# A retention layer and its MLP: the state cleared by VectorE, and a new order for the early tasks

## The chip, the cores and the metric

The kernel runs on one core of a Trainium2 chip. The metric is the device time of one execution in microseconds; of several executions the median counts. A profile is one execution recorded by the hardware: it shows when each instruction of each engine started and how long it took. The engines are TensorE (PE, matrix products), VectorE (DVE), ScalarE (ACT), GpSimd (POOL) and SyncE (SP, here only an issuer of transfers). They run side by side and wait for each other through semaphores. Matmuls write to PSUM banks; everything else is in SBUF.

## The reference

Two layers, one after the other. The first is a retention layer over 4 batches, 8 heads, 768 steps and head width 64; each head decays its state by its own factor:

```python
for t in range(S):
    state = gamma[None, :, None, None] * state + np.einsum('bhd,bhe->bhde', k[:, :, t], v[:, :, t])
    y[:, :, t] = scale * np.einsum('bhd,bhde->bhe', q[:, :, t], state)
```

with `gamma = 1 - 2**(-5 - h)` and `scale = 1/sqrt(64)`. Its output, with the heads side by side, is x (4 x 768 x 512). The second layer normalises each row of x and sends it through an MLP:

```python
xn = (x - mu) / np.sqrt(var + 1e-06) * g_ln
ch = np.maximum(xn @ w_ch1, 0.0) @ w_ch2
return (x + ch).astype(np.float32)
```

w_ch1 is 512 x 2048, w_ch2 is 2048 x 512.

## The kernel before

**Tiles.** The 768 steps of a batch are cut into 6 chunks of 128. A tile t is one chunk c of one batch b, with all heads. The 24 tiles come in the order of `TILES` (line 190): tiles 0 to 3 are chunk 0 of the four batches, 4 to 8 are chunks 1 to 5 of batch 0, and so on. Retention is computed chunk by chunk. Within a chunk it is a masked product of q and k with v; what earlier chunks hand on is a state per head, 64 x 64, kept for all heads in two alternating tiles `state[0]` and `state[1]` of 128 x 512 bf16 (line 275). Only the two diagonal blocks of each pair of heads are ever written, so the rest of both tiles must be zero: `c_zero` (line 339) clears them once.

**The steps of a tile**, by the names used below (t is the tile, the engine in brackets):
- tk, tq (PE, lines 498, 505): k and q are transposed into the banks b0 and b1. trk (ACT, 256) and trq (DVE, 510, scaled by decay) copy them out. From tile 8 on a DMA transpose takes the place of tk and tq.
- pa (PE, 538): the product of trk and trq. asb (DVE, 562): pa times the decay mask.
- y (PE, 586, and 582 for what comes from the state): asb times v.
- bn (DVE, 601 and 602): mean and variance of each row of y. xn (DVE, 613): y less its mean, times g_ln. x_all (ACT, 619): a copy of y, which reads its bank after xn.
- tx (PE, 672): xn is transposed. xnt (ACT, 256) copies it out for the MLP.
- vg (POOL, 633), pd (PE, 645) and the state update (DVE, 659, two instructions): v with decay, its product with k summed in PSUM, and the scaled sum put into a state tile. Tile t of chunk c needs the update of chunk c - 1 of its batch.
- Sqrt (ACT, 694) and the reciprocal (DVE, 700) give 1/sigma, which is needed only when the MLP's result is added.

**The MLP.** Tiles are taken in groups: eight of one tile, four of two, two of four. The first product, m1(g, n), runs over quarter n of group g's hidden width (line 719; 16 matmuls of 128 x 128 for a group of one tile) into one of two buffers named mm; a relu (line 732 on ACT, 734 on DVE) empties it into h1. Quarter n uses the part w1_n of the first weights. The second product (line 757, m2) takes h1 into a bank and line 767 adds x.

**What sets the order.** Each step is a task, made by `plan.add` in `Plan` (line 86) and numbered as it is made. `ORDER` (lines 29 to 69) lists all 866 tasks; each engine takes its own in that order and never passes a waiting one. Where a number is 10000 or more, the ten thousands digit picks the second engine that may do the task and the hundred thousands digit the second bank. `Plan.order` walks the list with planned durations and landing times (`w_pad` is one of these: ns added to the planned landing of a weight load). From its planned starts `Plan.fill` (line 145) puts matmuls on zeros (line 785) into the gaps that it expects on TensorE before 14 us, to keep TensorE busy. By its arithmetic there are 25 of these, the last ahead of y of tile 1.

**Loads.** GpSimd issues the loads of q, k, v (line 430) and of the weights (line 438) in one queue; each casts from fp32 to bf16. k and q of tile 0 come in by SyncE's and ScalarE's queues and are cast by ScalarE and VectorE (line 256). From tile 9 on small copies by GpSimd (line 447) hold a load back until an earlier one has landed.

**Where the clear stands.** Task 13 (`zerod`, line 359) is on GpSimd, behind the load of w1_2 and ahead of vg of tile 0. The first state update (216) waits for it.

Of the kernel before, what the change touches and what calls it, by code (L numbers as in the profile page):

```python
# [14 lines left out]
PE, ACT, DVE, POOL, SP = range(5)  # L15
# [4 lines left out]
              "k3", "q3", "v3", "w1_2", "k4", "q4", "v4", "k5", "q5", "v5", "w1_3", "w2_0",  # L20
              "k6", "q6", "v6", "k7", "q7", "v7", "w2_1", "w2_2", "w2_3"],
    "bufs": {"qsb": 6, "ksb": 5, "vsb": 9, "qk": 8, "tr": 6, "vg": 3, "trq": 3, "trk": 3},
    "load_pad": 600, "w_pad": 1500, "lead": 32, "lead2": 32, "sq_at": 28000, "late_load": 1700, "two": 4, "m2b": ("b0",), "m2all": 16, "inter": 4, "every": 4, "tail": (0, 384, 512), "step": 8, "pace": 8, "ahead": 3,
    "slack": 600, "tr_pad": 4000, "x_pad": 3500, "vg_pad": 2500, "fill": 0.8, "fill_end": 14000,
}

ORDER = [int(x) for x in """
16 17 2 0 3 19 20 23 14 8 15 1 24 5 7 9 25 4 10 6 21 11 26 18 22 146 45 100147 149 148  # L30
27 150 28 151 153 46 162 100163 29 152 154 164 165 30 155 12 166 31 156 167 32 157 158
159 47 168 176 13 524 169 179 214 100177 170 525 33 215 178 171 172 216 180 34 173 181
532 35 526 36 533 182 37 190 527 534 183 193 38 100191 184 535 48 192 185 186 194 187
195 49 540 542 541 196 204 543 528 197 39 207 100205 198 536 529 40 200 42 43 41 206 544
50 217 234 52 51 53 10537 55 208 100224 54 199 201 545 550 209 225 548 551 210 227 44
226 251 202 549 552 228 218 56 211 546 553 547 222 275 212 219 538 229 235 220 100241
554 539 530 10555 221 213 242 244 531 243 230 231 556 560 57 174 557 258 561 245 261 236
232 233 558 100237 562 238 246 259 247 10559 260 566 563 564 567 262 252 570 203 248 249
254 565 188 255 568 60 250 569 263 100722 160 61 58 59 268 62 287 253 298 63 723 716 724
301 66 264 67 64 717 65 725 269 718 161 571 175 189 719 265 726 266 720 576 100271 270  # L40
276 307 267 578 272 579 577 239 728 273 68 69 278 277 72 729 730 731 318 73 279 70 299
71 280 580 572 732 281 300 282 74 322 284 223 286 734 735 75 288 581 283 285 736 302 303
290 289 573 737 291 738 574 319 584 292 740 741 293 320 294 296 742 308 304 240 585 78
575 743 582 744 295 297 310 333 79 76 309 77 339 586 305 583 311 80 746 587 334 747 312
335 313 314 274 316 323 81 256 315 748 84 350 749 351 588 592 317 325 85 82 83 379 750
589 257 324 354 326 727 602 86 752 87 753 327 328 329 603 593 590 754 755 594 591 330 90
331 340 352 332 342 756 341 343 721 380 598 321 599 595 91 758 336 759 344 760 761 596
733 88 345 89 355 762 346 368 348 353 600 92 757 745 739 337 597 347 93 764 96 349 97 94
381 601 95 765 98 338 357 604 356 766 606 386 99 605 382 607 767 358 306 359 383 614 612
768 360 384 615 361 613 363 770 397 102 771 103 100 362 772 398 365 364 763 369 101 104  # L50
371 370 773 403 610 372 608 774 611 373 776 616 609 399 366 105 374 387 108 109 617 375
618 414 367 377 106 107 777 620 418 751 376 378 389 619 110 388 778 390 779 622 415 391
385 404 780 392 393 621 623 630 782 395 111 114 429 115 631 394 112 400 456 113 433 626
116 624 117 396 406 120 121 416 405 430 783 627 625 407 784 431 408 628 419 409 634 785
410 629 632 411 412 457 118 119 122 413 421 635 786 445 633 420 123 788 126 458 422 127
789 646 124 423 424 790 425 427 647 401 125 426 428 791 642 638 434 436 792 435 794 795
796 639 643 465 769 437 438 640 417 439 440 442 128 797 459 641 129 441 446 443 476 132
644 798 432 402 133 645 636 130 448 447 648 131 134 138 637 460 650 449 450 649 800 651
461 451 452 801 802 477 454 803 444 775 480 462 453 466 478 455 135 491 804 136 137 468
492 467 806 139 495 807 469 470 140 493 808 471 141 809 472 142 474 473 475 652 653 654  # L60
481 483 482 484 810 655 656 658 143 510 479 485 144 787 506 805 657 799 145 659 660 661
486 662 507 496 487 489 664 663 488 508 490 666 498 497 665 499 667 668 670 669 500 671
501 502 672 673 504 511 812 674 503 505 676 513 512 675 514 678 463 677 680 515 679 682
813 681 814 683 516 494 811 509 517 781 519 464 518 520 815 100830 831 816 521 832 818
819 200824 820 825 684 817 793 685 826 690 688 691 827 689 694 696 833 695 522 686 697
687 708 709 821 698 699 692 693 523 822 848 700 828 834 702 100842 701 703 706 707 704
200836 714 837 705 715 712 838 849 843 713 710 711 850 844 845 839 846 851 840 100854
852 855 856 823 847 841 835 829 853 857 860 861 858 862 863 864 859 865
""".split()]


# [90 lines left out]
def kernel(  # L162
# [16 lines left out]
    nc = tc.nc  # L179
# [158 lines left out]

    def c_zero(eng):
        for x in state:  # L340
            nc.gpsimd.memset(x, 0.0)

    a = plan.add
    small = a(DVE, 1200, -100, c_small)
# [11 lines left out]
    qscd = a(ACT, 700, -91, c_qsc, [args, table])  # L356
    maskd = a(DVE, 1230, -50, c_mask, [vscd, tri])
    gchd = a(ACT, 900, 100, c_gch, [small, qscd, vscd], at=9000)
    zerod = a(POOL, 500, 0, c_zero, at=9000)
    exps = [gchd, qscd, vscd]  # L360

    def c_gb(eng):
# [101 lines left out]
    for g in range(NG):  # L464
        for ho in range(HO):
            unit["1", g, ho] = u
            u += GROUPS[g] / 4
            every = CFG["every"] if GROUPS[g] == 1 else 8 if 12 <= G0[g] < 16 and GROUPS[g] == 2 else 4
# [239 lines left out]
    for g in range(NG):  # L708
        n = GROUPS[g]
        hb, h0 = buf_of[g]  # L710
        two = GMAX // n
# [109 lines left out]
```

## Time and profile before

| | before |
|---|---|
| median of 5 runs | 215.87 us (215.34 to 217.04) |
| profiled execution, its own time | 217.04 us |
| span from its first to its last instruction | 215.3 us |
| TensorE busy | 206.8 us, 96% |
| VectorE, ScalarE, GpSimd busy | 119.6, 86.4, 97.0 us |
| mean granted clock of TensorE | 0.999 |
| first layer of the MLP, line 719 | 896 matmuls, 95.2 us |
| second layer, line 757 | 379 matmuls recorded, 88.4 us |
| matmuls on zeros, line 785 | 24 recorded, 8.0 us |
| clear of the state, line 341 | 2 on GpSimd, 1.01 us, from 14.14 us |

The profiled execution was the slowest of the five. A few matmul records are missing from a trace, so counts on TensorE can be a little low. In a timeline a row is a run of instructions of one line: start, time from the first start to the last end, engine, line, what it writes and reads, how many, and in brackets how long the engine was idle before it and what ended that. Matmuls overlap, so the time from one row's start to the next says more about cost than the time of a row. Busy TensorE counts from issue to drain in the same way.

### The profile page before, as it was taken

To read this page: it belongs to the slowest core of one execution; us is meant where nothing else is said; L and a number is where in the kernel's file an instruction comes from. 1 tells how busy PE (TensorE), PEld (TensorE's weight loads), DVE (VectorE), ACT (ScalarE), POOL (GpSimd) and SP (SyncE) were. 2 spreads that over 40 slices of the span, in tenths; PEclk is the share of its full clock that TensorE was granted. 3 is DMA by queue.
4 is the path that set the end of the run, shared out by engine and by line. 5 is a ranking of instruction groups with operands and counts; after the bars stand their busy time and mean duration, and the time that the engine had idled before them with its cause. 6 is when DMAs were issued, how large, how long until landed. Compare 5 with 4: busy or idle time off the path is not lost.

```text
span 215.3 us, 4941 instructions
## 1 busy us (share of the span) xinstructions
PE 206.8 (96%) x2005; PEld 131.8 (61%) x2027; DVE 119.6 (56%) x260; ACT 86.4 (40%) x175; POOL 97.0 (45%) x151
## 2 busy tenths in 40 slices
PE   7998899999999999999999999999999999999992
PEld 3368799994666667665676776674445444444452
DVE  5477667872667774863684677478686510030041
ACT  5246678652412324343333542261366601544200
POOL 8968697529778475755675648221000000000000
PEclk9999999999999999999999999999999999999999
DMA  9999999999999999999999999939440260000035
GB/s 128 168 180 180 165 191 178 205 114 117 105 112 128 122 128 171 142 261 158 88 172 165 105 170 121 151 73 125 98 155 20 56 191 3 0 0 0 0 144 200
DMA packets 108890, 26.85 MB, mean 125 GB/s; under 512 B 101569, under 2 KB 105921, under 8 KB 108866
## 3 DMA queue, kind: packets, MB, share of 16 engines
q0 software_dynamic: 77024, 13.37, 82.0%
q1 hardware_dynamic: 27186, 6.59, 21.9%
q10 hardware_dynamic: 4656, 6.56, 8.8%
q8 instruction: 16, 0.26, 0.5%
q14 instruction: 8, 0.07, 0.1%
HBM read 27.30 MB, written 6.29 MB: 156 GB/s over the span
## 4 chain that ended last, share of the span: by engine, by line
PE 91%; ACT 2%; DMA 2%; DVE 2%; issue 1%; ACTq 0%; DVEq 0%
PE b L757 38%; PE mm L719 38%; PE pa L538 3%; PE pd L645 2%; DMA osb<-in_q_dram 2%; PE pd L785 2%; PE b L572 2%; PE b L548 2%; PE mm L364 1%; PE b L586 1%; PE b L498 1%; DVE xn L613 1%; PE b L505 1%; DVE bns L601 1%; PE b L672 1%
## 5 line engine op out<-in xcount | busy, mean ns | idle before, releaser
L719 PE MATMUL mm<-xnt,w 128*128 128x128 bf16 (+2 forms) x896 | 95.2, 257 | 0.9 <-ACT xnt L256 0.8
L757 PE MATMUL b<-w,h 128*128 128x512 bf16 (+2 forms) x379 | 88.4, 370 | 1.2 <-issue 0.2
L732 ACT ACTIVATE h<-mm 128x512 bf16<-128x512 f32 x93 | 55.0, 598 | 83.6 <-PE mm L719 83.3
L719 PEld LDWEIGHTS <-w 128*128 128x128 bf16 x896 | 66.1, 98 | 21.3 <-issue 1.0
L757 PEld LDWEIGHTS <-h 128*128 128x128 bf16 x400 | 37.0, 98 | 37.7
L562 DVE TENSOR_TENSOR asb<-pa,mask 128x1024 bf16<-128x1024 f32 x24 | 29.4, 1224 | 21.0 <-PE pa L538 20.5
L767 DVE SCALAR_TENSOR_TENSOR osb<-b,rstd,x_all 128x512 f32<-128x512 f32 (+2 forms) x25 | 18.0, 727 | 27.3 <-PE b L757 27.0
L601 DVE BATCH_NORM_STATS2 bns<-b 128x6 f32<-128x256 f32 (+1 forms) x40 | 17.8, 477 | 17.7 <-PE b L572 11.0
L619 ACT CAST x_all<-b 128x256 bf16<-128x256 f32 (+1 forms) x40 | 16.2, 417 | 23.1 <-DVE xn L613 18.9
L613 DVE SCALAR_TENSOR_TENSOR xn<-b,mv,gb 128x256 bf16<-128x256 f32 (+1 forms) x40 | 20.1, 532 | 0.8
L633 POOL TENSOR_TENSOR vg<-vsb,vsc 128x512 bf16<-128x512 bf16 x16 | 16.6, 1049 | 7.8 <-PE pd L645 7.5
L430 POOL DMA_DIRECT2D vsb<-in_v_dram x20 | 18.1, 905 | 2.1 <-DMA qsb<-in_q_dram 1.3
L659 DVE TENSOR_TENSOR state<-pd,gch 64x256 bf16<-64x256 f32 x40 | 16.6, 414 | 3.4 <-PE pd L645 2.6
L430 POOL DMA_DIRECT2D qk<-in_q_dram x16 | 14.2, 887 | 2.4 <-issue 2.4
L430 POOL DMA_DIRECT2D qk<-in_k_dram x16 | 14.3, 892 | 1.2 <-issue 1.1
L447 POOL COPY scrap<-qk 1x1 bf16<-1x1 bf16 x30 | 5.8, 192 | 19.1 <-DMA qk<-in_q_dram 10.5
L700 DVE RECIPROCAL rstd<-rstd 128x1 f32<-128x1 f32 (+2 forms) x14 | 2.0, 157 | 13.4 <-ACT rstd L694 13.4
L785 PE MATMUL pd<-zeros 128*128 128x512 bf16 (+1 forms) x24 | 8.0, 487 | 1.3 <-DVE zeros L291 1.2
L438 POOL DMA_DIRECT2D w<-in_moe_w_ch_dram x8 | 6.2, 776 | 4.0 <-DMA w<-in_moe_w_ch_dram 4.0
L572 PEld LDWEIGHTS <-asb 128*128 128x128 bf16 x128 | 5.8, 98 | 2.4
L447 POOL COPY scrap<-vsb 1x1 bf16<-1x1 bf16 x15 | 2.6, 176 | 9.5 <-DMA vsb<-in_v_dram 9.4
L527 DVE TENSOR_TENSOR trq<-tr,qsc 128x512 bf16<-128x512 bf16 x16 | 6.7, 418 | 0.1
(68 smaller groups left out, 130.2 us busy)
## 6 DMA issues: line engine op xcount, KB each, us to landing
out_dram<-osb ACTq DMA_DIRECT2D x23, 256.0 KB, 3.4
w<-in_moe_w_ch_dram POOLq DMA_DIRECT2D x8, 512.0 KB, 10.3
vsb<-in_v_dram POOLq DMA_DIRECT2D x20, 128.0 KB, 5.2
qk<-in_k_dram POOLq DMA_DIRECT2D x16, 128.0 KB, 4.5
qk<-in_q_dram POOLq DMA_DIRECT2D x16, 128.0 KB, 5.1
qsb<-in_q_dram POOLq DMA_DIRECT2D x7, 128.0 KB, 9.2
v<-in_v_dram POOLq DMA_DIRECT2D x4, 128.0 KB, 7.7
ksb<-in_k_dram POOLq DMA_DIRECT2D x4, 128.0 KB, 9.2
```

Source lines behind the costliest of these rows:

```text
L430: nc.gpsimd.dma_start(out=tile_of(kind, j), in_=src)
L562: nc.vector.tensor_tensor(out=take("asb", t, [P, NPAIR, 2, P], BF16).rearrange("p i a t -> p a i t"), in0=held["pa", t], in1=mask.rearrang ...
L601: nc.vector.bn_stats(out=bns[:, t, i, :], in_=x)
L613: nc.vector.scalar_tensor_tensor(out=dst, in0=src, scalar=mv[:, t, 0:1], in1=g, op0=ALU.subtract, op1=ALU.mult)
L619: nc.scalar.copy(out=dst, in_=src)
L633: e.tensor_tensor(out=take("vg", j, [P, H, D], BF16), in0=tile_of("v", j), in1=vsc[:, cc, :].unsqueeze(2).to_broadcast([P, H, D]), op=ALU. ...
L659: nc.vector.tensor_tensor(out=held["pb", n][o, :, o], in0=held["pd", b][o, :, o], in1=gch[o, cc, :].unsqueeze(2).to_broadcast([D, NPAIR, D ...
L719: nc.tensor.matmul(p[:, j, :], lhsT=w1[:, ko, (ho + j) * P:(ho + j + 1) * P], rhs=held["xnt", hb][:, h0:h0 + n, ko, :], start=(ko == 0), s ...
L732: nc.scalar.activation(out=dst, in_=src, func=AF.Relu)
L757: nc.tensor.matmul(held[key][:, 0:w], lhsT=held["h1", hb][:, ho, i * P:(i + 1) * P], rhs=w2[:, ho, cols], start=(ho == 0), stop=(ho == HO ...
L767: nc.vector.scalar_tensor_tensor(out=take("osb", key, [P, w], FP32), in0=held[key][:, 0:w], scalar=rstd[:, t:t + 1], in1=x_all[:, t, cols] ...
L785: nc.tensor.matmul(held["pd", "warm"][:, 0:w], lhsT=zeros[:, 0:P], rhs=zeros[:, 0:w], start=True, stop=True)
```

## The change

It has three parts.

1. The clear of the two state tiles is made by VectorE instead of GpSimd, and its task stands behind the making of the causal triangle (task 6) and ahead of the cast of q of tile 0 (task 21). GpSimd goes from the load of w1_2 straight to vg of tile 0.
2. `w_pad` goes from 1500 to 550.
3. `ORDER` is new for the first tasks, most of it up to tile 8 (the last to move is a Sqrt, 256, in the time of tile 10); after that both lists are the same. No task is added or left out. Per engine:

- TensorE. From tq of tile 2 on, before: tq2, pd of tile 0 (215), tx1, pa2, m1(1,0) (532), m1(0,1) (526), y2, tk3, m1(1,1) (534), tq3, tx2, pa3, m1(2,0) (540), m1(2,1), y3, tk4, m1(0,2), tq4, m1(1,2), tx3. After: tq2, tx1, pa2, 532, 215, y2, 534, tk3, 526, tq3, tx2, pa3, 540, m1(2,1), y3, tk4, m1(1,2), tq4, m1(0,2), tx3. Up to tq2 nothing moves. From tile 4 to tile 7 steps of the chain and matmuls of the MLP change places with neighbours.
- ScalarE. The decay factors of the state (task 12, line 337) stand ahead of the copy of g_ln's rows and of trk1, where they stood behind them. The first Sqrt, which also loads the table for it, was 202 (group 3), behind trk of tile 5; it is now 160 (group 0), between xnt of tile 0 and trk of tile 2. The other Sqrts are spread out behind it. The relu of m1(0,0) (525) goes behind xnt1. For tiles 2 and 3 xnt goes ahead of x_all. Some relus change between ScalarE and VectorE: 527, 529, 549, 531 and 561 to VectorE, and 537, 555 and 559 to ScalarE.
- VectorE. The first state update (216) stood between trq2 and asb2; it now stands behind asb3. Of the reciprocals, 161 (group 0) goes ahead of trq3. The later state updates of batch 0 change places with neighbours.
- GpSimd. Besides the clear, vg of tile 7 (268) goes ahead of the issue of q of tile 9, behind which it stood.

```diff
@@ CFG @@
...
-    "load_pad": 600, "w_pad": 1500, "lead": 32,
+    "load_pad": 600, "w_pad": 550, "lead": 32,
...
@@ ORDER @@
-16 17 2 0 3 19 20 23 14 8 15 1 24 5 7 9 25 4 10 6 21 11 26 18 22 146 45 100147 149 148
-27 150 28 151 153 46 162 100163 29 152 154 164 165 30 155 12 166 31 156 167 32 157 158
-159 47 168 176 13 524 169 179 214 100177 170 525 33 215 178 171 172 216 180 34 173 181
-532 35 526 36 533 182 37 190 527 534 183 193 38 100191 184 535 48 192 185 186 194 187
-195 49 540 542 541 196 204 543 528 197 39 207 100205 198 536 529 40 200 42 43 41 206 544
-50 217 234 52 51 53 10537 55 208 100224 54 199 201 545 550 209 225 548 551 210 227 44
-226 251 202 549 552 228 218 56 211 546 553 547 222 275 212 219 538 229 235 220 100241
-554 539 530 10555 221 213 242 244 531 243 230 231 556 560 57 174 557 258 561 245 261 236
-232 233 558 100237 562 238 246 259 247 10559 260 566 563 564 567 262 252 570 203 248 249
-254 565 188 255 568 60 250 569 263 100722 160 61 58 59 268 62 287 253 298 63 723 716 724
-301 66 264 67 64 717 65 725 269 718 161 571 175 189 719 265 726 266 720 576 100271 270
-276 307 267 578 272 579 577 239 728 273 68 69 278 277 72 729 730 731 318 73 279 70 299
-71 280 580 572 732 281 300 282 74 322 284 223 286 734 735 75 288 581 283 285 736 302 303
-290 289 573 737 291 738 574 319 584 292 740 741 293 320 294 296 742 308 304 240 585 78
...
+16 17 2 0 3 19 20 23 14 8 15 1 24 5 7 9 25 4 10 6 13 21 11 26 18 45 22 27 146 28 149
+100147 148 150 46 29 151 30 162 100163 153 12 152 165 154 164 166 155 31 156 157 167 32
+158 168 169 47 100176 159 170 524 177 178 160 179 100172 214 180 181 171 173 532 33 215
+182 183 525 184 534 161 190 533 193 34 35 36 526 100191 186 535 192 194 10527 187 540 37
+38 185 542 195 48 196 49 39 541 216 197 204 40 42 43 41 536 198 50 217 543 207 234
+100205 206 528 537 200 52 51 201 544 199 208 10529 224 209 545 552 188 548 10549 553 174
+100225 210 227 550 551 546 53 55 175 226 228 211 54 212 44 218 219 547 213 554 530 220
+555 251 202 221 235 100241 229 538 230 56 244 10531 236 556 539 242 275 231 558 100258
+557 232 559 243 560 10561 237 562 57 245 246 233 238 239 563 222 566 259 564 247 260 567
+248 189 261 570 262 252 565 568 249 60 254 255 250 569 223 253 203 263 100722 61 268 58
+59 62 287 298 63 723 716 724 301 66 67 64 717 65 264 725 269 718 571 719 265 726 266 270
+720 576 100271 276 307 267 578 272 579 577 728 273 68 69 278 277 72 729 730 731 318 73
+279 70 299 71 280 580 572 732 281 300 282 74 322 284 286 734 735 75 288 581 283 285 736
+302 303 290 289 573 737 291 738 574 319 584 292 740 741 293 320 294 296 742 308 304 240
...
@@ c_zero and its task @@
     def c_zero(eng):
         for x in state:
-            nc.gpsimd.memset(x, 0.0)
+            nc.vector.memset(x, 0.0)
...
     gchd = a(ACT, 900, 100, c_gch, [small, qscd, vscd], at=9000)
-    zerod = a(POOL, 500, 0, c_zero, at=9000)
+    zerod = a(DVE, 480, -94, c_zero)
     exps = [gchd, qscd, vscd]
```

(A leading 100 as in 100172 puts that transpose into bank b1 instead of b0; some of these change too. 176 is tk2, 177 tq2, 172 tx1, 180 pa2, 182 y2, 190 tk3, 191 tq3, 186 tx2, 194 pa3, 196 y3, 204 tk4.)

## The prediction

> **What bounds the kernel now.** I first read the page's busy shares and forty slices, then the waits of TensorE, then the timelines of the engines in the first 36 us.
>
> ```profile
> PE 206.8 (96%) x2005; PEld 131.8 (61%) x2027; DVE 119.6 (56%) x260; ACT 86.4 (40%) x175; POOL 97.0 (45%) x151
> ...
> PE   7998899999999999999999999999999999999992
> ```
>
> TensorE (PE) is busy 206.8 of 215.3 us. The 8.5 us that it isn't lie at the start, in slices 3 to 5 (about 11 to 27 us) and in the last one, where the output leaves. The change touches no matmul's shape and nothing in the tail, so it can only win what PE loses early. The waits of TensorE, for the first 60 us and then for the rest:
>
> ```profile
> PE mm L719 <- ACT xnt L256: 0.8, 2, 0.4
> PE b L672 <- DVE xn L613: 0.7, 2, 0.4
> ...
> PE b L757 <- issue: 0.2, 1, 0.2
> ```
>
> The columns are total us, count, longest. Twice in the first 60 us PE waits for xn (the normalised tile) and twice for its transposed copy; after 60 us it waits for nothing worth naming. In TensorE's timeline (start, us, bracket: idle before):
>
> ```profile
> 17.30 0.40 PE L672 MATMUL b<-idn,xn 128*128 128x128 bf16 x4 [0.30 <-DVE xn L613]
> 17.63 0.40 PE L538 MATMUL pa<-trq,trk 64*128 64x128 bf16 x8
> 18.40 1.95 PE L719 MATMUL mm<-xnt,w 128*128 128x128 bf16 x32 [0.38 <-ACT xnt L256]
> 20.18 0.40 PE L586 MATMUL b<-v,asb 128*128 128x64 bf16 x8
> ...
> 22.45 0.40 PE L672 MATMUL b<-idn,xn 128*128 128x128 bf16 x4 [0.41 <-DVE xn L613]
> ...
> 23.55 1.95 PE L719 MATMUL mm<-xnt,w 128*128 128x128 bf16 x32 [0.37 <-ACT xnt L256]
> 25.33 0.40 PE L586 MATMUL b<-v,asb 128*128 128x64 bf16 x8
> 25.57 0.39 PE L498 MATMUL b<-idn,ksb 128*128 128x128 bf16 x4
> ...
> 33.36 0.40 PE L645 MATMUL pd<-vg,ksb 128*128 128x128 bf16 x4
> 33.89 1.95 PE L719 MATMUL mm<-xnt,w 128*128 128x128 bf16 x32
> ```
>
> Here one tile's chain (y at 20.18, statistics, xn, transpose, copy, first MLP matmul at 23.55) is longer than the matmuls set beside it. At 33.36 the step lasts 0.53 us instead of the usual 0.22, so 0.31 is lost. VectorE and ScalarE:
>
> ```profile
> 3.09 0.28 DVE L327 TENSOR_SCALAR cm<-fidx,pos 128x128 f32<-128x128 f32 x1
> 4.85 0.29 DVE L256 CAST qsb<-osb 128x256 bf16<-128x256 f32 x1 [1.48 <-DMA osb<-in_q_dram]
> ...
> 17.49 0.85 DVE L659 TENSOR_TENSOR state<-pd,gch 64x256 bf16<-64x256 f32 x2
> 18.37 1.23 DVE L562 TENSOR_TENSOR asb<-pa,mask 128x1024 bf16<-128x1024 f32 x1
> ```
> ```profile
> 14.48 0.58 ACT L256 COPY xnt<-b 128x512 bf16<-128x512 bf16 x1 [0.47 <-PE b L672]
> 15.69 0.58 ACT L256 COPY trk<-b 128x512 bf16<-128x512 bf16 x1 [0.63 <-PE b L498]
> ...
> 31.76 1.28 ACT L694 ACT_TABLE_LOAD   x1
> 33.06 0.29 ACT L694 ACTIVATE rstd<-mv,epsb 128x1 f32<-128x1 f32 x1
> ```
>
> The table load for Sqrt, 1.28 us, sits just ahead of that 0.31: ScalarE's relu comes at 33.26 instead of 31.76, and the mm buffer it frees is what the matmul at 33.89 takes. On GpSimd the clear, and (window on one issue; last number is us to landing) the load of k4:
>
> ```profile
> 14.14 1.01 POOL L341 MEMSET state<- 128x512 bf16 x2
> ```
> ```profile
> ksb<-in_k_dram POOLq DMA_DIRECT2D x1, 128.0 KB, 9.1
> ```
>
> k4, issued at 16.09, lands at 25.22. Read in the same way q3 lands at 21.59, w1_2 (issued 13.40) at 24.25 and q4 at 26.19. Loads of 128 KB land about 0.9 us apart, eight to eleven us after their issue: the transfers queue, so the time of issue doesn't set the landing.
>
> **What the skill says.** "VectorE: DVE Perf Modes", section "Zero memsets can be issued as uint32 (trn2)": a zero clear of bf16 can run on half as many elements; the trace agrees, zeros (128x512 bf16) shows as 256 uint32 in 0.27 us. "SBUF — State Buffer", section "Who interferes with whom": a VectorE instruction with at most one SBUF input outside the two-port modes doesn't contend with GpSimd, so the new clears should not hold up the loads issued beside them; no run here shows it yet. "ScalarE: Activation LUTs", section "What ACT_TABLE_LOAD costs": 1283 ns plus a drain of 1380 ns. The trace agrees with the first (1.28) and shows no second: the Sqrt starts 0.02 us after the load ends. "TensorE: Matmul & The Clock Gate", section "What's actually happening": PE falls to half rate after an idle window of about 3.4 us. Here 4 transposes take 0.61 us until 10.5 us and 0.40 from 14.05 on; no fall is seen after.
>
> **The change part by part.**
>
> *Clear on VectorE.* Two clears at 0.27 (row of zeros) are 0.54; unhalved, two of about 0.5 (GpSimd's 1.01 for the pair) are 1.0. They start at 3.37, end at 3.9 to 4.4, inside the 1.48 us wait for q (4.85). Cost 0; without that cover 0.54 to 1.0, onto the mask. GpSimd gains 1.01 us before its product vg0 and the loads from k4 on. These queue anyway: gain 0, at most 1.0 earlier landings (rival 3).
>
> *w_pad 1500 to 550.* It is a planned landing delay. With the order written out it can only change the fills' widths; those stand before tasks up to 168 (y of tile 1), which wait for no weights and aren't moved. Same 25 fills, cost 0.
>
> *Decay factors (12) earlier on ScalarE.* Five activations, 0.58 us, from 11.18 to about 6.3, into 3.82 us of idle. Cost 0.
>
> *First Sqrt (160) at 14.96 on ScalarE.* Load 1.28 plus 0.29 end at 16.55 to 16.65 (the trace's 31.76 to 33.35), so trk2 moves from 15.69 to about 16.55 and ends at 17.13. Its reader, pa2 at 17.63, has 0.5 to spare. Behind trk2, x_all1 waits for xn1 (17.24) as before, and xnt1 keeps 17.76 because relu 525 now goes behind it. Cost 0 with that 0.5 of cover. At 33.9 the load is gone and relu 549 goes to VectorE: 0.31 won.
>
> *Order.* In tile 2's stage state update 216 leaves VectorE between trq2 and asb2, and its matmul 215 goes behind 532. I walk it with row durations, PE steps start to start (16 MLP matmuls 0.89, transposes 0.22, y 0.24, pa 0.33) and 0.05 for a signal:
> - asb2 starts when pa2 ends, 18.03 + 0.03 = 18.06 (before 18.37), ends 19.29.
> - PE: 532 at 18.40, 215 at 19.29, y2 at 19.51 (before 20.18: 526 stood there). Tile 1's two waits stay; the first becomes about 0.5, as 215 no longer fills it.
> - 534, tk3, 526 follow; tq3 at 19.51 + 0.24 + 0.89 + 0.22 + 0.89 = 21.75. q3 (21.59) is there by 0.16.
> - xn2 ends 2.21 after y2's start as before: 21.72. So its transpose goes at 21.97 without a wait (before 22.45).
> - trq3 waits for tq3: 22.19 to 22.61. pa3 at 22.66, a new wait of 0.45 on PE. xnt2 (22.42 + 0.58) ends 23.00, 540 at 23.06 (before 23.55).
> - y3 at 23.06 + 2 x 0.89 = 24.84, tk4 could go at 25.08 (0.49 ahead) but k4 lands at 25.22: 25.27, before 25.57. **0.30 won, 0.19 given back to the load.**
>
> The same walk over the old order gives 25.49 for tk4, against 25.57 traced. From there each PE step has its inputs 0.1 us or more early (next tightest: tq4 at 26.38, q4 26.19), until 33.6, where the 0.31 above is won. The sum is 0.61; since the walk of the old order was 0.08 fast at tk4, I take 0.55. After 50 us the two orders differ in small ways (vg7 ahead of q9's issue, which goes some 1.2 us later; tile 9's q is read at 65.5 and lands at 55.3, about ten us early), cost 0.
>
> **Sum.** Span 215.3 - 0.55 = 214.75. The profiled execution took 217.04, 1.74 more than its span, and is the slowest of the five shown; against the median, 215.87 - 0.55 = 215.3.
>
> **Rivals.**
> 1. *Nothing comes of it.* tk4 is held by a landing. If k4 lands 0.3 later, or the Sqrt detour is longer than the 0.5 of cover, the stage's gain is gone. With the skill's drain of 1.38, trk2 ends at 18.5, pa2 slips 0.9, and y3 comes near 26.0, 0.67 late; less the 0.31 at 33.6 it is +0.35: 216.2. For: 0.13 us of slack is all that q3 has. Against: the trace shows no drain. Range 215.7 to 216.3.
> 2. *The clock falls (slower).* PE's waits near 17 us grow to about 0.5 and 0.4 within 1.5 us. Should its clock drop there, one window of 3.4 us at half rate loses 1.7; less 0.55 it is +1.15: 217.0. It decides once a drop lasts over 1.1 us. Against: the gap is far below the window that the skill names, and old gaps of 0.41 and 0.37 did nothing.
> 3. *More is won.* If GpSimd's free 1.01 us brings k4 in sooner, tk4 goes at 25.08: 0.49 + 0.31 = 0.80, so 215.1. Tile 1's and pa3's waits would have to go too (another 0.3 or more) to pass 1.08. For: w1_2 landed just ahead of k4. Against: landings 0.9 apart don't look like issue times.
>
> **How the numbers follow.** 0.5% is 1.08 us, about what a measurement of this kernel can tell from no change; the five runs before span 1.7. My forecast of 0.55 lies inside it. Chances: forecast 0.55 (own range 214.7 to 215.9), rival 1 0.18, rival 2 0.12, rival 3 0.15. Faster by over 0.5%: 0.13 (0.10 from rival 3 with more than I priced, 0.03 from scatter). Slower: 0.13 (0.11 from rival 2, 0.02 from rival 1). Between: 0.74. The range 214.4 to 216.5 takes in rival 1 and most of rival 3.
>
> **What would show it.** VectorE's clears near 3.4 us, and q's cast still at 4.85. A table load near 15.0 on ScalarE with pa2 still at 17.6. y2 near 19.5; the transpose near 22.0 with no wait; a wait of about 0.45 ahead of pa3; y3 near 24.85, tk4 at about k4's landing; no 0.3 gap near 33.6; the first second-layer matmul near 47.85 instead of 48.40. The prediction is wrong if pa2 moves past 18, if matmuls double in length after 17 us, if a wait for mm appears after 26 us, or if tk4 goes more than 0.3 ahead of or behind 25.27.

## The result and the profile after

| | before | after |
|---|---|---|
| median | 215.67 us (80 runs, 214.26 to 220.65) | 214.92 us (43 runs, 213.91 to 216.58) |
| profiled execution, its own time | 217.04 us | 214.4 us |
| span | 215.3 us | 212.6 us |
| ratio of times, 95% interval | | 0.997 (0.9956 to 0.9984) |

The ratio is 0.65 us (0.003 of 215.67) of gain, with an interval from 0.35 to 0.95 us; forecast were 0.55 us and a time of 215.3. It is within half a per cent of no change, and the interval leaves no change out. The medians are of all runs, while the ratios, here and below, leave out the few that are over 1.5% above the fastest of the same kernel, so the two can differ by a tenth of a per cent.

The two spans differ by 2.7 us, four times as much. Most of that is not the change. How soon TensorE reaches its full rate differs between executions, also of the kernel before (below, with w_pad alone). The waits of TensorE in the first 60 us of the changed kernel, and the first part of its timeline, show the early course:

```profile
PE b L672 <- DVE xn L613: 0.5, 1, 0.5
...
PE b L498 <- DMA k<-in_k_dram: 0.5, 1, 0.5
...
PE mm L719 <- ACT xnt L256: 0.4, 1, 0.4
PE pa L538 <- DVE trq L510: 0.4, 1, 0.4
...
PE b L498 <- DMA ksb<-in_k_dram: 0.3, 1, 0.3
```
```profile
6.06 0.81 PE L785 MATMUL pd<-zeros 128*128 128x512 bf16 x3
...
8.19 0.40 PE L498 MATMUL b<-idn,k 128*128 128x128 bf16 x4
...
14.58 0.40 PE L672 MATMUL b<-idn,xn 128*128 128x128 bf16 x4 [0.52 <-DVE xn L613]
14.91 0.40 PE L538 MATMUL pa<-trq,trk 64*128 64x128 bf16 x8
15.68 1.05 PE L719 MATMUL mm<-xnt,w 128*128 128x128 bf16 x16 [0.37 <-ACT xnt L256]
16.57 0.39 PE L645 MATMUL pd<-vg,k 128*128 128x128 bf16 x4
16.80 0.40 PE L586 MATMUL b<-v,asb 128*128 128x64 bf16 x8
...
18.61 0.40 PE L498 MATMUL b<-idn,k 128*128 128x128 bf16 x4 [0.52 <-DMA k<-in_k_dram]
...
19.73 0.39 PE L505 MATMUL b<-idn,qsb 128*128 128x128 bf16 x4
19.95 0.39 PE L672 MATMUL b<-idn,xn 128*128 128x128 bf16 x4
20.70 0.40 PE L538 MATMUL pa<-trq,trk 64*128 64x128 bf16 x8 [0.36 <-DVE trq L510]
...
22.83 0.40 PE L586 MATMUL b<-v,asb 128*128 128x64 bf16 x8
23.07 0.39 PE L498 MATMUL b<-idn,ksb 128*128 128x128 bf16 x4
```

Three fills (the matmuls on zeros) take 0.81 us here; in the first profile of before they took 1.49, and what stands behind them was slower too. So k of tile 1 is transposed at 8.19 instead of 10.06, and all that follows is about two us earlier, in work that the change doesn't touch. I call this the early course, and that of before's first profile the late one. What the change did is seen in the order and the waits: pd (L645) and y (L586) directly behind one m1 step, the transpose of xn at 19.95 without a wait, a new wait of 0.36 us for trq3, and two waits for loads (k3 and, at 34.67, k6) which the first profile of before did not have. tk4 follows y3 at the usual 0.24 us, so here no load holds it; k4 had landed 0.09 us before. On VectorE and ScalarE:

```profile
3.38 0.54 DVE L341 MEMSET state<- 128x256 uint32 x2
4.87 0.29 DVE L256 CAST qsb<-osb 128x256 bf16<-128x256 f32 x1 [0.95 <-DMA osb<-in_q_dram]
```
```profile
11.69 0.59 ACT L256 COPY xnt<-b 128x512 bf16<-128x512 bf16 x1
12.30 1.28 ACT L694 ACT_TABLE_LOAD   x1
13.59 0.29 ACT L694 ACTIVATE rstd<-mv,epsb 128x1 f32<-128x1 f32 x1
13.79 0.56 ACT L256 COPY trk<-b 128x512 bf16<-128x512 bf16 x1
```

The clears take 0.54 us and leave 0.95 us of the wait for q. The table load and the Sqrt take 1.58 us, and trk2 is copied 0.56 us ahead of pa2 (14.35 and 14.91).

### The profile page after: what moved, and what is told of

It reads as the page before. It is cut to its first block, busy times and chain, and to the rows that moved or that the text cites. A ratio compares the mean times of both kernels' runs of the same rounds, so it can differ in the third digit from the quotient of the medians.

```text
span 212.6 us, 4939 instructions
## 1 busy us (share of the span) xinstructions
PE 203.7 (96%) x2005; PEld 130.3 (61%) x2027; DVE 121.4 (57%) x264; ACT 85.2 (40%) x173; POOL 96.1 (45%) x149
## 4 chain that ended last, share of the span: by engine, by line
PE 82%; DMA 10%; POOL 5%; issue 1%; DVE 0%; POOLq 0%
PE b L757 39%; PE mm L719 34%; DMA ksb<-in_k_dram 5%; DMA w<-in_moe_w_ch_dram 5%; PE pa L538 2%; PE pd L645 2%; PE b L572 2%; POOL v L430 2%; PE b L548 2%; POOL k L430 1%; POOL qsb L430 1%; POOL w L438 1%; PE b L586 0%; PE b L672 0%; PE b L582 0%
## 5 line engine op out<-in xcount | busy, mean ns | idle before, releaser
L732 ACT ACTIVATE h<-mm 128x512 bf16<-128x512 f32 x91 | 53.8, 598 | 81.4 <-PE mm L719 81.1
L785 PE MATMUL pd<-zeros 128*128 128x512 bf16 (+1 forms) x24 | 6.6, 420 | 1.3 <-DVE zeros L291 1.2
L430 POOL DMA_DIRECT2D qsb<-in_q_dram x7 | 6.3, 899 | 1.7 <-DMA k<-in_k_dram 1.3
## 6 DMA issues: line engine op xcount, KB each, us to landing
ksb<-in_k_dram POOLq DMA_DIRECT2D x4, 128.0 KB, 10.1
```

The costliest lines, as they stand in the source:

```text
L430: nc.gpsimd.dma_start(out=tile_of(kind, j), in_=src)
L732: nc.scalar.activation(out=dst, in_=src, func=AF.Relu)
```

## The experiments

Four theories were put to the test. A is the prediction's: the gain is the stage up to tk4 plus the wait for mm near 33.6 us. B: k6's landing holds TensorE at tk6 in most executions, and the gain is made there. C: the clear on GpSimd delays vg0, and with it pd0. D: landings decide from execution to execution how much of the stage's gain is kept, and the order of tiles 4 to 7 brings the rest.

All kernels compute the whole result. Timed against before on the same chip:

| kernel | median, us | before, us | ratio (95%) |
|---|---|---|---|
| before, w_pad 550 | 215.52 | 215.6 | 0.9999 (0.9967 to 1.0031) |
| before, first Sqrt moved | 215.24 | 215.6 | 0.9973 (0.9946 to 1.0001) |
| before, order of tiles 2 and 3 | 215.49 | 215.6 | 0.9982 (0.9953 to 1.0012) |
| before, tk6 moved | 215.66 | 215.6 | 0.9991 (0.9966 to 1.0016) |
| before, clear on VectorE | 215.76 | 215.34 | 1.0020 (0.9993 to 1.0047) |
| after, clear back on GpSimd | 214.56 | 215.34 | 0.9947 (0.9923 to 0.9971) |
| after, ScalarE late | 215.63 | 215.34 | 1.0010 (0.9989 to 1.0032) |
| after, k6 and q6 ahead of w2_0 | 214.43 | 215.34 | 0.9950 (0.9929 to 0.9972) |
| before, both parts | 215.56 | 215.51 | 1.0004 (0.9976 to 1.0032) |
| before, new order from tk4 on | 215.25 | 215.51 | 0.9998 (0.9981 to 1.0016) |
| after, table load back | 214.81 | 215.51 | 0.9957 (0.9935 to 0.9978) |
| before, k6 and q6 ahead of w2_0 | 215.7 | 215.51 | 1.0014 (0.9987 to 1.0041) |

The intervals are some 0.5 us to each side, so a part of 0.3 us can't be resolved by time. The profiles can, because TensorE repeats itself: from the start of the first matmul of the second layer (m2, about 46 to 48 us) to the start of its last one it takes 162.88 to 162.90 us in thirteen of the fourteen profiles, and 163.25 in the other (order of tiles 2 and 3). Behind its last matmul 3.4 to 4.0 us remain, in no order that follows the kernels. So what counts is when m2 begins, and that splits at tk4. In us, with k4's landing in the same profile:

```
                              tk4 after k4's landing   tk4 to m2
before, first profile                  0.35              22.83
before, w_pad 550                      0.05              23.27  (waits for k6)
before, clear on VectorE               0.42              22.83
before, tk6 moved                      0.51              22.83
before, k6 and q6 ahead of w2_0        0.42              22.83
before, first Sqrt moved               0.40              22.55
before, order of tiles 2 and 3         1.58 (late course) 22.83
before, new order from tk4 on          2.37 (late course) 22.55
before, both parts                     0.04              22.56
after                                  0.09              23.00  (waits for k6)
after, clear back                      0.05              22.56
after, table load back                 0.05              22.56
after, k6 and q6 ahead of w2_0         0.05              23.07  (waits for w1_3)
after, ScalarE late                    0.15              22.55
```

In the two profiles marked with the late course k4 had long landed when TensorE came to tk4. Before's first profile has the late course too, but there k4 also landed late (25.22 us; 22.97 to 24.51 in the others).

**w_pad alone.**

```diff
-    "load_pad": 600, "w_pad": 1500,
+    "load_pad": 600, "w_pad": 550,
```

> The kernel before with w_pad 550 alone. Theory A (the prediction): the same instructions in the same order, so 0.0 us against before, and what it shows is scatter: under 0.4 us. Theory B (k6's landing holds TensorE ahead of tk6 in most executions) says 0.0 too. A third theory, that the result is nothing but how soon TensorE speeds up, lets this kernel differ from before as much as the changed kernel does, 0.7 us. In the profile, if TensorE's transposes take 0.40 us from about 5 us on rather than from 14 us on, the span should be about 2 us shorter than the 215.3 of the first profile, with nothing changed.

The ratio is 0.9999, and the matmuls on zeros that both profiles hold have the same widths: nothing in the program has changed. Yet this profile has a span of 213.6 us and the early course; so 1.7 of the 2.7 us come with no change of order at all. It also shows a wait that the first profile did not have, and what it waits for:

```profile
13.64 0.39 PE L505 MATMUL b<-idn,qsb 128*128 128x128 bf16 x4
14.59 0.38 PE L645 MATMUL pd<-vg,k 128*128 128x128 bf16 x4 [0.56 <-POOL vg L633]
14.81 0.39 PE L672 MATMUL b<-idn,xn 128*128 128x128 bf16 x4
```
```profile
12.43 1.10 POOL L341 MEMSET state<- 128x512 bf16 x2
13.38 1.16 POOL L633 TENSOR_TENSOR vg<-v,vsc 128x512 bf16<-128x512 bf16 x1
```

**The first Sqrt alone.**

```diff
-... 30 155 12 166 31 156 167 32 157 158 159 47 168 ... 170 525 33 ... 34 173 181
+... 30 155 12 166 31 156 167 32 157 158 159 160 47 168 ... 170 33 ... 34 173 525 181
```

> The kernel before with the first Sqrt (160) between xnt0 and trk2 on ScalarE and relu 525 behind xnt1; nothing else. Theory A: pa2 doesn't move and the wait for mm near 33.6 us goes: -0.3 us. Theory B: in executions in which k6's landing holds tk6, the 0.3 won ahead of it or beside it is lost at the load: 0.0 to -0.1 us. Rival 1 of the prediction (the detour is longer than its cover): +0.3 us or more, and pa2 later than its neighbours.

About 0.6 us by the ratio, with an interval that just reaches no change. The profile is plainer: pd to the next m1 step takes 0.24 us,

```profile
32.16 0.40 PE L645 MATMUL pd<-vg,ksb 128*128 128x128 bf16 x4
32.40 1.78 PE L719 MATMUL mm<-xnt,w 128*128 128x128 bf16 x29
```

and with the Sqrt at its old place (the kernel with the clear alone moved) 0.53 us:

```profile
31.48 0.40 PE L645 MATMUL pd<-vg,ksb 128*128 128x128 bf16 x4
32.01 1.95 PE L719 MATMUL mm<-xnt,w 128*128 128x128 bf16 x32
```

tk4 to m2 is 22.55 instead of 22.83. That is A's 0.31, as 0.28, and it reaches the second layer.

**The order of tiles 2 and 3 alone.**

```diff
-170 525 33 215 178 171 172 216 180 34 173 181 532 35 526 36 533 182 37 190 527 534 183 ...
-194 187 195 49 540 542 541 196
+170 525 33 178 171 172 180 34 173 181 532 215 35 36 533 182 534 37 190 526 183 ...
+194 187 10527 195 49 540 542 541 216 196
```

> The kernel before with the order of tile 2 and 3 from the changed kernel: 216 behind asb3, 215 behind 532, y2, then 534, tk3, 526, and relu 527 on VectorE; Sqrt, clear and all of tile 4 on as before. Theory A: y2 comes 0.65 us sooner, tk4 0.2 to 0.3 sooner, and that reaches the end: -0.25 us. Theory B: y2 and tk4 come sooner by as much, but tk6 waits for k6 at the same time: 0.0 us.

The time is 0.4 us lower by the ratio, with no change inside the interval. This profile happens to have the late course of before's first profile, so the two can be laid side by side:

```profile
18.35 1.05 PE L719 MATMUL mm<-xnt,w 128*128 128x128 bf16 x16 [0.37 <-ACT xnt L256]
19.24 0.39 PE L645 MATMUL pd<-vg,k 128*128 128x128 bf16 x4
19.46 0.40 PE L586 MATMUL b<-v,asb 128*128 128x64 bf16 x8
...
21.93 0.39 PE L672 MATMUL b<-idn,xn 128*128 128x128 bf16 x4
22.60 0.40 PE L538 MATMUL pa<-trq,trk 64*128 64x128 bf16 x8 [0.29 <-DVE trq L510]
...
25.18 0.39 PE L498 MATMUL b<-idn,ksb 128*128 128x128 bf16 x4
```

y2 at 19.46 (worked out: 19.51; before: 20.18), tx2 at 21.93 (21.97; 22.45), pa3 at 22.60 after a wait (22.66; 22.78), tk4 at 25.18 (25.08 without a wait for k4, 25.27 with it; 25.57). k4 landed at 23.60 in this execution, so the load held nothing back. m2 begins at 48.02, in before's first profile at 48.40.

**tk6 alone.**

```diff
-220 100241 554 539 530
+220 554 539 530 100241
```

> The kernel before with one task moved: tk6 (241) two MLP matmul steps later, behind 554 and 530. Theory A: TensorE doesn't wait at tk6, as in the first profile, where k6 landed 0.75 us ahead: 0.0 us. Theory B: in executions in which k6 is late for TensorE, up to 1.8 us of matmuls now stand ahead of that wait: -0.7 us in these, -0.4 to -0.7 us in the median.

No change (0.9991). B wanted 0.4 us or more; the interval (0.7 us faster to 0.3 slower) doesn't rule that out by itself. In the profile k6 landed 2.36 us ahead of the moved tk6, and it would have been in time at the old place too.

**The clear alone.**

```diff
-            nc.gpsimd.memset(x, 0.0)
+            nc.vector.memset(x, 0.0)
-    zerod = a(POOL, 500, 0, c_zero, at=9000)
+    zerod = a(DVE, 480, -94, c_zero)
```

with 13 behind 6 in the list.

> The kernel before with the clear alone moved to VectorE (task 13 behind task 6, ahead of q's cast); all else in the old order. Theory A (the prediction): the two clears take 0.54 us inside VectorE's wait for q, GpSimd's free time only lets loads queue longer: 0.0 us. Theory C: where TensorE speeds up early, its pd0 waits about 0.56 us for vg0, which GpSimd makes behind the clear (seen in the profile with w_pad alone, where tx1 then goes at 14.81 instead of 14.58); with the clear gone vg0 comes about 1 us sooner and that wait goes: -0.2 us. Rival 3 (loads land sooner by up to 1 us): -0.3 us or more, and k4 lands sooner after w1_2 than 0.95 us.

1.0020, with no change inside and C's 0.2 us just outside (0.15 us faster to 1.0 slower). The wait of pd0 for vg0 is gone from the profile and tx1 goes at 14.46, but at 18.73 k3's load holds TensorE by 1.0 us, so the 0.2 us is not there in the end. k4 lands 0.97 us after w1_2, as in before (0.97): nothing landed sooner, which was rival 3.

**The changed kernel with the clear back on GpSimd.**

```diff
-            nc.vector.memset(x, 0.0)
+            nc.gpsimd.memset(x, 0.0)
-    zerod = a(DVE, 480, -94, c_zero)
+    zerod = a(POOL, 500, 0, c_zero, at=9000)
```

with 13 behind 47 again.

> The changed kernel with the clear put back on GpSimd, behind the load of w1_2; all else as changed. Theory A and C: pd0 now stands behind 532 and has over 2 us of room for vg0, so the clear costs nothing there: -0.6 us against before, the same as the changed kernel. Rival 3: the loads from k4 on land up to 1 us later and the gain shrinks to about -0.3 us.

0.9947: the gain is all there without the clear's move. The interval overlaps with that of the changed kernel, so that it is better isn't shown.

**ScalarE made late.**

```diff
+                for _ in range(4 if g == 0 else 0):
+                    nc.scalar.copy(out=wait_dst, in_=zeros[:, 0:2 * P])
                 nc.scalar.activation(out=rstd[:, s], in_=mv[:, s, 1], func=AF.Sqrt, bias=epsb,
```

> The changed kernel with four copies of 128x256 bf16 into a scratch tile put ahead of the first Sqrt on ScalarE: about 1.38 us more, the drain of rival 1 made real. Theory A: the 0.5 us of cover is used up, pa2 slips about 1.0 us, y2 1.1 to 1.2 us, and with a k4 that still lands at its time tk4 slips 0.4 to 0.9 us, so the whole gain is lost: 0.0 to +0.4 us against before. Theory B (the loads of k4 and k6 set the pace and TensorE waits for them anyway): y2 slips as much but tk6 does not: -0.6 us against before, as without the copies.

The copies took 1.73 us and the gain is gone (1.0010), as A says; B's 0.6 us lies outside the interval. TensorE waits for the copy of trk2, which still has the bank, and once more further on:

```profile
14.41 0.39 PE L507 MATMUL b<-idn,qsb 128*128 128x128 bf16 x4
15.88 0.38 PE L674 MATMUL b<-idn,xn 128*128 128x128 bf16 x4 [1.09 <-ACT trk L256]
...
19.09 0.39 PE L588 MATMUL b<-v,asb 128*128 128x64 bf16 x8 [0.87 <-DMA v<-in_v_dram]
```

(The added lines shift the line numbers by two.) The place is tx1 and not pa2 as expected: tx1 takes trk2's bank. In the changed kernel trk2 ends at 14.35 and tx1 starts at 14.58, so the cover is 0.23 us and not 0.5. That the copies cost the gain is shown by the times. This one profile doesn't show it: y2 waits for v2, which landed at 19.05, and would have waited for it without the copies as well. So that m2 begins at 47.22 here and at 46.07 in the changed kernel's profile is not their doing alone.

**k6 and q6 ahead of w2_0, in the changed kernel and in before.**

```diff
-48 ... 49 39 ... 40
+48 ... 39 ... 40 49
```

> The changed kernel with one load moved: w2_0 goes behind k6 and q6 in GpSimd's queue, so that k6 and q6 land about 2.5 us sooner and w2_0, which is first read near 46 us, about 1.9 us later. Theory A: no wait at tk6 in most executions, -0.6 us against before, as the changed kernel. Theory B: the wait of 0.28 us that the changed kernel's profile shows at tk6 goes, -0.3 us more: -0.9 us against before.

> The kernel before with w2_0 behind k6 and q6 in GpSimd's queue; k6 and q6 land about 2.5 us sooner. Theory A: TensorE isn't held at tk6: 0.0 us. Theory B: it is held there in most executions, -0.6 us. Theory D: it is held there in two of eight walks, by 0.6 to 0.7 us: -0.15 us in the mean.

In before nothing changes (1.0014), although k6 lands at 30.85 and TensorE reaches tk6 at 34.32, as in the other early profiles of the old order (34.24 to 34.63). B's 0.6 us lies outside that interval. In the changed kernel, with only 7 runs, it is 0.9950, which can't be told from the 0.9947 with the clear back or from 0.997. Theory B falls: k6 holds TensorE in two of the fourteen profiles (w_pad's and the changed kernel's, within 0.05 us of its landing) and not in most. There it costs 0.44 us on the way from tk4 to m2, in either order.

**Both parts, and what is left.** In the first, the edits of the two single parts together; in the second, the old list up to tk4 and then the new one, with

```diff
+227 160 ... 238 188 174 ... 248 161 175
```

for the Sqrts of the first groups and their reciprocals.

> The kernel before with both parts on which the prediction's sum rests and no more: the order of tile 2 and 3 and the first Sqrt with relu 525 moved. Theory A (stage up to tk4, and the wait for mm that the table load causes): all of the gain, -0.5 us or more. Theory D (the load's landings decide, execution by execution, how much of the stage's gain is kept, and the rest of the gain lies in the order of tiles 4 to 7): the row durations walked over the landings of eight profiled executions give 0.0 to -0.64, -0.25 us in the mean.

> The complement: the kernel before up to tk4 (old order of tile 2 and 3, clear on GpSimd), and the new order of all engines from tk4 on; the first Sqrt and its table load stay behind trk of tile 5, as before. Theory A: nothing of the stage's gain, and with the table load at its old place no more than the 0.3 us of the wait for mm, which goes only if relu 549's move to VectorE is what ends it: 0.0 to -0.3 us. Theory D: in all eight walks -0.31 or more, -0.89 in the two in which k6 lands late: -0.45 us in the mean.

The times decide nothing between A and D: 1.0004 and 0.9998, medians 0.05 us above and 0.26 below. By A alone the first should have been 0.5 us or more faster, and that lies at the edge of its interval (-0.5 to +0.7 us); by D the second should have been 0.45 us faster, and that lies just outside its interval (-0.4 to +0.3). The first one's profile has both parts in place: tk4 0.04 us after k4's landing and 22.56 us to m2. In that execution the loads themselves came late (k2 held TensorE by 1.2 us and v2 by 0.7, k4 landed at 24.15), as they did in some profiles of either order. The second has 22.55, with the table load at its old place.

**The table load back.** The same edit of the Sqrts in the changed kernel.

> The changed kernel with the first Sqrt and its table load back behind trk of tile 5 (the Sqrts of groups 1 and 2 and their reciprocals go behind them); relu 549 stays on VectorE. If the table load itself made the wait for mm near 33.6 us, it comes back: -0.3 us against before. If the relu's place behind it on ScalarE made it, and VectorE does that relu now, nothing is lost: -0.6 us against before, as the changed kernel.

0.9957: nothing is lost. The table load is back ahead of ScalarE's relus, but VectorE has done the relu that stood behind it:

```profile
29.27 0.69 DVE L734 TENSOR_SCALAR h<-mm 128x512 bf16<-128x512 f32 x1 [0.89 <-PE mm L719]
```
```profile
29.47 1.28 ACT L694 ACT_TABLE_LOAD   x1
30.77 0.29 ACT L694 ACTIVATE rstd<-mv,epsb 128x1 f32<-128x1 f32 x1
30.97 0.58 ACT L732 ACTIVATE h<-mm 128x512 bf16<-128x512 f32 x1
```

tk4 to m2 is 22.56. And y3 was so early here that its successor waited for the load:

```profile
22.18 0.40 PE L586 MATMUL b<-v,asb 128*128 128x64 bf16 x8
23.26 0.40 PE L498 MATMUL b<-idn,ksb 128*128 128x128 bf16 x4 [0.69 <-DMA ksb<-in_k_dram]
```

## Why the prediction was right

**Bound.** Held: TensorE bounds the kernel and from m2 on nothing moves (162.9 us in all). One reading was loose: the page's slices below nine tenths are 1, 4, 5 and 40, not 3 to 5.

**Clear at no cost.** Held: 0.54 us inside the wait for q, and the clear alone is not faster. The loads issued beside it start at 3.24 and 4.10 us in both first profiles, so VectorE's clears don't hold them up. That GpSimd's time is worth nothing was argued from queued loads. For the loads that is right (0.97 us from w1_2 to k4 in either case). It overlooked a wait: where TensorE is early, pd0 waits about 0.4 to 0.7 us for vg0, which stands behind the clear. Either half of the change ends it, the clear's move or pd0's; in the one profile with the clear alone moved a load took the gain back.

**w_pad and the fills at no cost.** Held (0.9999).

**The Sqrt's detour.** The cost of nothing held, but its cover was read from the wrong reader: 0.5 us up to pa2, where tx1 takes the bank after 0.23. That did no harm because no drain is seen: the table load ends at 13.58 and the Sqrt starts at 13.59. On this the Trainium skill ("ScalarE: Activation LUTs", section "What ACT_TABLE_LOAD costs") adds 1.38 us of drain to every switch, and the trace doesn't agree. 1.73 us more on ScalarE cost all of the gain.

**The stage up to tk4, 0.30.** Held in its steps, with some luck in the size. The steps came within 0.1 us of the worked times where the course was the same. In the five profiles with the new order of tiles 2 and 3 and the early course (ScalarE late apart), tk4 goes 0.04 to 0.09 us after k4's landing. In the five with the old order and the early course it goes 0.40 to 0.51 after it in four and 0.05 in one. So 0.35 to 0.46 us can be won in four of these and nothing in the fifth, 0.31 in the mean. That a load is what ends the gain is seen in four of the five profiles with the new order, where TensorE stands until k4 has landed; in the changed kernel's own it doesn't. The forecast of 0.30 was worked out for one execution of the late course with a late k4 (0.49 less 0.19 for the load); that other executions with other landings give the same mean was not to be known from it.

**The wait for mm, 0.31.** The size held (22.83 to 22.55, so 0.28). The cause was only half told. The prediction named the table load and the relu's move together; the runs show that each way is enough: the table load moved with the relu on ScalarE (22.55), or the table load in place in the new order from tk4 on, in which relu 549 is on VectorE (22.55 and 22.56). It is one gain and not two. The relu's move without the rest of that order was not run.

**Inputs ready from tk4 on.** This failed in part. Read from one late execution it looked as if only k4 came late. In the eleven profiles of the early course k2 or k3 holds TensorE by 0.5 to 1.2 us in nine, v2 by another 0.6 to 0.9 in four of these, and, behind tk4, k6 holds it in two and w1_3 in one (where the order of the loads was changed). The waits ahead of tk4 stand in both orders; that they change the difference little is argued, not shown. For k6 it isn't so, as follows.

**The sum.** 0.31 and 0.28 make 0.59, forecast 0.61 less 0.08, measured 0.65 (0.35 to 0.95). Yet the two parts put into before did not show that gain in time (1.0004, and 0.59 lies just outside the interval), while every kernel with the whole new order and no added work did (0.9947 to 0.997). So the agreement of the sum doesn't prove that these two parts are all of it.

The traces hold one thing that the prediction has no term for. Where no load holds it, tk6 follows tk4 by 10.27 us with the two parts alone and by 11.16 to 11.17 in the whole new order, while m2 comes equally soon (22.56). k6 landed 10.1 to 11.7 us after k4 in the twelve profiles with k6's load at its place. With tk4 right behind k4, the old place of tk6 would have been held up in six of these, by 0.29 us in the mean of the twelve, and the new one in one, by 0.04. In the profile with the table load back k6 landed 10.98 after k4 and TensorE didn't wait; at the old place it would have, by 0.7 us. In before, with tk4 0.4 behind k4, the same arithmetic gives 0.08. By this estimate from the landings the two parts alone are worth 0.38 us and the whole order 0.63, and both lie inside the intervals measured. It is theory D in a milder form: the later tk6 keeps what the early steps won. No experiment isolates it, so this stays open.

**Rivals.** Rival 1's drain is in no profile here, but 1.73 us of other work in its place cost about what it said (0.2 us slower than before, between 0.2 faster and 0.7 slower). Its slack for q3 should read 0.16 as in the walk, and q3 held nothing in any profile. Rival 2, a fall of the clock near 17 us, is in no profile: four transposes of 128x128 take 0.38 to 0.40 us from 14.5 us on in all of them. Rival 3's sooner landings are in none: k4 lands 0.94 to 0.97 us after w1_2 in all fourteen.

## What to carry to other kernels

When one engine is busy nearly all the time, find the first instant from which it never waits again; only what comes before it can be won, and a gain there can end at the next thing that arrives by its own clock, here a queued load. So look at each such arrival further on too: a step moved ahead meets the next load earlier. One profile is one execution: compare waits in several, and measure a step from the event that paces it (a landing) rather than from the start. If two edits end the same wait, they are worth it once.

## What was not expected of the hardware

TensorE's full rate comes at different times in executions of one program. Three fills of 128x512 near 6 us took 0.81 us in nine of fourteen profiles, 0.96 and 1.36 in one each and 1.49 in three, before's first among them; k of tile 1 was then transposed at 8.07 to 8.52 us or, in the three, at 10.04 to 10.06 us. What decides it the runs don't show. The landing of the first weights, issued at 4.97 us in before's first profile and in the changed kernel's, ranged from 11.2 to 13.1 us over the profiles. k4, nine loads later, landed 11.1 to 12.2 us after them, so the offset is kept only in part. A stop of about one us in the queue of loads also shows at other places, ahead of k3 in several profiles. Much of the scatter of the times probably comes from these; that was not measured.
